# A fused attention and gated-MLP block: how its first rows are normalised, and where two weight loads stand in the queue

## The chip, the cores and the metric

One core of one Trainium2 chip. The metric is the device time of one execution in microseconds (us); the median of several runs is compared. A core has five engines that run side by side, each through its own instructions in the order in which the program lists them: TensorE (PE, matmuls), VectorE (DVE), ScalarE (ACT), GpSimd (POOL) and SyncE (SP, which here issues nearly all DMAs).

## The reference

The input x has 2048 rows of 640. Each row is normalised (mean and variance over its 640 values); everything else works on the normalised rows xn:

```
xn  = (x - mean) / sqrt(var + 1e-5)
# attention in 4 segments of 512 rows, 32 heads of 20, with a memory M, z carried on
q, k, v = xn @ wq, xn @ wk, xn @ wv
p     = softmax(q k^T * scale + mask)            # within a segment
a_mem = (phi(q) M) / (phi(q) z + 1e-6)           # from the segments before
o     = sigmoid(beta) * a_mem + (1 - sigmoid(beta)) * (p v)
M, z += phi(k)^T v, sum phi(k)                   # phi(t) = t + 1 if t > 0 else exp(t)
s   = o @ wo
# gated MLP, inner width 1536
h   = sigmoid(xn @ w_gate) * (xn @ w_up)
out = x + s * silu(h @ w_down)
```

## The kernel before

Work goes segment by segment, 512 rows each (n = 0 to 3). A segment's rows come as four blocks of 128 rows (j = 0 to 3), two to a tile xt2 that has two buffers. For matmuls the kernel needs xn transposed (xnT, five chunks of 128 columns). `Wg` and `Wu`, the gate and up weights, are loaded in three blocks of 512 columns (`load_glu(i, 0)` and `load_glu(i, 1)`, 640 KB each, issued by SP); one block serves four gates or four ups of 128 columns.

Two kinds of code set the order. From segment 0's scores on a planner interleaves attention (`scores`, L516; `weigh`, L534) with due tasks and with `bulk`, the list of gates, ups and downs. What comes ahead of that is written out by hand in `startup` (L573). Every engine keeps the program's order, and SP's DMAs go out in program order too.

`startup` begins with 40 small matmuls on an identity (`warm`, L571), which keep TensorE busy while the first rows arrive. For each of segment 0's four blocks `ln_stats` (L227) takes mean and variance on DVE (two `bn_stats` over 320 columns each, L236 and L237, and an aggregate, L238), and POOL makes the inverse root (add eps L241, power -0.5 L242). `ln_norm` (L248) then normalises on DVE (L253), transposes by five matmuls on PE into one PSUM tile (L260), and ACT copies it out to xnT (L261). As soon as two blocks are there, V's matmuls start (`v_tile`, L356: five matmuls for half the columns of one block; the six half tiles of blocks 0 to 2 are made here). Then come K's five chunks (`k_chunk`, L289) and Q's (`q_chunk`, L321), each five matmuls into one of three PSUM buffers that ACT empties.

K and Q then change their layout through DRAM. `stage_out` (L310) writes three or two chunks of K to the scratch tensor Ks (of Q to Qs); `relay` (L274) reads them back as four DMAs into KT (QT), head by head. `q_bound` makes a bound on the scores that goes the same way through Cs (L345) and is read back by `c_in` (L353) as four DMAs into QT. The first scores need KT, QT from Qs and QT from Cs. Between Q and these scores PE has eight gates and ups, which use block 0 of Wg and Wu; the next ones need block 1. The loads of block 1 stand at L614 and L615, behind the first QT<-Cs issues. The next transposes of segment 1 (by DMA, L263), block 2 of the weights, and the second half's relays follow in the same queue. A DMA's landing semaphore is one of eight that are used in turn, so a DMA waits until the eighth one before it has landed.

Of the kernel before, what the change touches and what calls it, by code (L numbers as in the profile page):

```python
# [9 lines left out]
P = 128  # L10
S = 2048
D = 640
# [17 lines left out]
ACT = mybir.ActivationFunctionType  # L30
ALU = mybir.AluOpType
# [18 lines left out]

NU = len(UNITS)
NSLOT = NG // 2 * NU
WARM = 40
FIRST = 0.45
PASS = [0.41, 0.41, 0.41, 0.2, 0.61]
R = NSLOT / 24
# [3 lines left out]
def kernel(  # L60
# [14 lines left out]
    nc = tc.nc  # L75
# [3 lines left out]
    cpool = ctx.enter_context(tc.tile_pool(name="const", bufs=1))  # L79
# [3 lines left out]
    lnp = ctx.enter_context(tc.tile_pool(name="ln", bufs=2))  # L83
    xpool = ctx.enter_context(tc.tile_pool(name="xpool", bufs=2))
# [4 lines left out]
    fpool = ctx.enter_context(tc.tile_pool(name="fpool", bufs=2))  # L89
# [35 lines left out]
    def later(lag, fn, *a):  # L125
        at(clock[0] + lag * R, 0.0, fn, *a)


    st = [dict() for _ in range(NSEG)]
# [31 lines left out]
    def load_glu(i, which):  # L161
        w, src = ((Wg, B_w_gate), (Wu, B_w_up))[which]
        nc.sync.dma_start(w[i][:], src[:, i * L:(i + 1) * L].rearrange("(c p) n -> p c n", p=P))
# [11 lines left out]

    nhalf = cpool.tile([P, 2], F32, name="nhalf")
    nc.gpsimd.memset(nhalf[:], -0.5)
    ident = cpool.tile([P, P], BF, name="ident")
    nc.gpsimd.memset(ident[:], 0.0)
    nc.gpsimd.affine_select(out=ident[:], in_=ident[:], compare_op=ALU.not_equal, fill=1.0,  # L180
# [46 lines left out]
    def ln_stats(n, p, i0=0, i1=2):  # L227
        s = st[n]
        x = s[f"x{p}"]
        if i0 == 0:  # L230
            s[f"mv{p}"] = lnp.tile([P, 2, 2], F32, name="mv")
            s[f"rstd{p}"] = lnp.tile([P, 2], F32, name="rstd")
        mv, rstd = s[f"mv{p}"], s[f"rstd{p}"]
        for i in range(i0, i1):
            bs = lnp.tile([P, 2, 6], F32, name="bs")
            nc.vector.bn_stats(bs[:, 0, :], x[:, i, 0:HB])  # L236
            nc.vector.bn_stats(bs[:, 1, :], x[:, i, HB:D])  # L237
            nc.vector.bn_aggr(mv[:, i, :], bs[:])  # L238

        def root():  # L240
            nc.gpsimd.tensor_scalar(rstd[:, i0:i1], mv[:, i0:i1, 1], EPS, None, op0=ALU.add)  # L241
            nc.gpsimd.tensor_tensor(rstd[:, i0:i1], rstd[:, i0:i1], nhalf[:, i0:i1], op=ALU.pow)  # L242
        if n <= 1:
            root()
        else:
            later(0.6, root)

    def ln_norm(n, p, i):  # L248
        s = st[n]
        if "xnT" not in s:  # L250
            s["xnT"] = xpool.tile([P, DC, L], BF, name="xnT")
        xn = lnp.tile([P, D], BF, name="xn")
        nc.vector.tensor_scalar(xn[:], s[f"x{p}"][:, i, :], s[f"mv{p}"][:, i, 0:1], s[f"rstd{p}"][:, i:i + 1],  # L253
                                op0=ALU.subtract, op1=ALU.mult)
        j = 2 * p + i
        dst = s["xnT"][:, :, j * P:(j + 1) * P]
        if n == 0:
            pT = dtile([P, DC, P], BF, "pT")
            for c in range(DC):
                nc.tensor.transpose(pT[:, c, :], xn[:, c * P:(c + 1) * P], ident[:])  # L260
            nc.scalar.copy(dst, pT[:])  # L261
        elif n == 1:
            nc.sync.dma_start_transpose(dst, xn[:])  # L263
        else:
            later(0.7, lambda: nc.sync.dma_start_transpose(dst, xn[:]))


    def half_tile(tiles, n, half):
        return tiles[(2 * n + half) % 3]

    def relay(n, half, src, dst):
        rows = src[n % 2].rearrange("(g r d) n -> r d g n", r=4, d=DH)
        for r in range(4):
            nc.sync.dma_start(half_tile(dst, n, half)[32 * r:32 * r + DH, :, :], rows[r][:, 4 * half:4 * half + 4, :])  # L274

    def evacuate(dst, ps):
        if delay[0]:
            nc.vector.tensor_copy(dst, ps)
        else:
            nc.scalar.copy(dst, ps)  # L280

    def k_chunk(n, c):
        s = st[n]
        if c == 0:
            s["k5"] = stg.tile([P, DC, L], BF, name="k5")
            s["kabs"] = stg.tile([P, DC], F32, name="kabs")
# [21 lines left out]
    def stage_out(n, half, src, dst, name):  # L308
        a, b = ((0, 3), (3, 5))[half]
        nc.sync.dma_start(src[n % 2][a * P:b * P, :].rearrange("(c p) n -> p c n", p=P), st[n][name][:, a:b, :])  # L310
        if n:
            later(1.0, relay, n, half, src, dst)
# [255 lines left out]
    def warm(count):  # L568
        ps = dtile([P, L], F32, "wps")
        for i in range(count):  # L570
            nc.tensor.matmul(ps[:, 0:P], lhsT=ident[:], rhs=ident[:], start=True, stop=True)  # L571

    def startup():  # L573
        warm(WARM)
        nc.gpsimd.memset(KT[0][:], 1.0)
        ln_stats(0, 0, 0, 1)
        ln_stats(0, 0, 1, 2)
        ln_norm(0, 0, 0)
        warm(10)
        ln_stats(0, 1, 0, 1)  # L580
        ln_norm(0, 0, 1)
        v_tile(0, 0, 0)
        ln_stats(0, 1, 1, 2)
        v_tile(0, 1, 0)
        ln_norm(0, 1, 0)
        v_tile(0, 0, 1)
        ln_norm(0, 1, 1)
        v_tile(0, 2, 0)
        v_tile(0, 1, 1)
        v_tile(0, 2, 1)  # L590
        v_ones(0, 4)
        make_ind()
        nc.gpsimd.memset(KT[1][:], 1.0)
        for c in range(DC):
            k_chunk(0, c)
        nc.gpsimd.memset(KT[2][:], 1.0)
        stage_out(0, 0, Ks, KT, "k5")
        for c in range(DC):
            q_chunk(0, c)
            if c == 0:  # L600
                stage_out(0, 1, Ks, KT, "k5")
                relay(0, 0, Ks, KT)
            elif c == 2:
                stage_out(0, 0, Qs, QT, "q5")
            if c < 2:
                ln_stats(1, 0, c, c + 1)
        make_bd()
        v_ones(4, 8)
        take(1)
        q_bound(0)  # L610
        relay(0, 0, Qs, QT)
        stage_out(0, 1, Qs, QT, "q5")
        c_in(0, (0,))
        load_glu(1, 0)  # L614
        load_glu(1, 1)  # L615
        ln_stats(1, 1, 0, 1)
        gates()
        take(1)
        ln_norm(1, 0, 0)
        ln_norm(1, 0, 1)  # L620
        take(1)
        ln_stats(1, 1, 1, 2)
        take(5)
        at(0.1, 0.68, v_tile, 0, 3, 0)
        at(0.5, 0.68, v_tile, 0, 3, 1)
        at(R * 2.0, 0.0, ln_norm, 1, 1, 0)
        at(R * 2.3, 0.0, ln_norm, 1, 1, 1)
# [118 lines left out]
    n = NSEG - 1  # L746
# [39 lines left out]
```

## Time and profile before

| | us |
|---|---|
| median of 3 runs | 338.39 (338.29 to 341.84) |
| the profiled execution | 339.99 |
| its span, first to last instruction | 338.3 |
| TensorE busy in it | 326.1 (96%) |
| VectorE, ScalarE, GpSimd busy | 223.9, 226.5, 111.0 |
| first warm matmul | 1.45 |
| first V matmul | 7.38 |
| first K matmul | 12.44 |
| first score matmul | 32.60 |

A row of the timeline gives the start, the length, the engine, the line, the operation, what it writes and reads, how many instructions are merged, and in brackets how long the engine was idle just before and what ended that. A q behind the engine's name (SPq, ACTq) marks its queue: issuing a DMA, not moving its data. When a DMA has landed is told by its semaphore, to which each DMA engine that carried a part of it adds a one. A matmul's end is modelled, so rows of PE overlap a little.

### The profile page before, as it was taken

Reading aid. Unit: us, or ns where it says so; the run is one execution under the profiler, and the core shown is the slowest. Engines: PE = TensorE matmul, PEld = TensorE weight load, DVE = VectorE, ACT = ScalarE, POOL = GpSimd, SP = SyncE. Lnnn points to the kernel's source line nnn. Section 1 sums busy time; section 2 is a strip of 40 time slices with the busy share of each in tenths; the row PEclk is TensorE's granted clock in tenths of the full one; section 3 lists DMA queues with packets and bytes.
Section 4 is the critical chain, followed back from the end, with each engine's and each line's share of the span. In section 5 each row is a group of like instructions: output and inputs, shape, how many; then the busy total and the mean of one; then the engine's idle time right before and its main releaser. Section 6 shows DMA issues by size and latency. Waiting matters only on the chain.

```text
span 338.3 us, 8318 instructions
## 1 busy us (share of the span) xinstructions
PE 326.1 (96%) x3360; PEld 186.5 (55%) x3402; DVE 223.9 (66%) x532; ACT 226.5 (67%) x237; POOL 111.0 (33%) x157
## 2 busy tenths in 40 slices
PE   8999899999999999999999999999999999999995
PEld 7544455445665565554566466554456655544673
DVE  6375356479877577778775977876673687533355
ACT  3653797778786666477876765565887776786730
POOL 6645232232325322332223622333222323233214
PEclk9999999999999999999999999999999999999999
DMA  7956994774840731045730263042220521210032
GB/s 237 343 183 194 265 112 83 234 214 91 186 109 3 131 92 53 20 137 88 203 94 2 54 105 98 21 155 86 74 70 3 83 76 41 63 55 3 2 62 78
DMA packets 54725, 35.53 MB, mean 105 GB/s; under 512 B 28576, under 2 KB 54688, under 8 KB 54688
## 3 DMA queue, kind: packets, MB, share of 16 engines
q1 hardware_dynamic: 52480, 32.23, 37.7%
q10 hardware_dynamic: 2208, 2.79, 2.7%
q8 instruction: 26, 0.43, 0.6%
q14 instruction: 11, 0.09, 0.1%
HBM read 20.19 MB, written 8.39 MB: 84 GB/s over the span
## 4 chain that ended last, share of the span: by engine, by line
PE 87%; DMA 5%; DVE 3%; ACT 2%; issue 1%; POOL 0%; SPq 0%; DVEq 0%; ACTq 0%; POOLq 0%
PE yp L456 14%; PE up L438 14%; PE gp L428 13%; PE Aps L547 9%; PE Sps L522 7%; PE sp L502 6%; PE psk L289 6%; PE psq L321 6%; PE psv L360 6%; DMA Wu<-in_B_w_up_dram 2%; PE wps L571 2%; DMA xnT<-xn 1%; PE dm L388 1%; PE am L410 1%; ACT pt L527 1%
## 5 line engine op out<-in xcount | busy, mean ns | idle before, releaser
L527 ACT ACTIVATE pt<-Sps 128x2048 bf16<-128x2048 f32 x80 | 150.1, 1876 | 24.6 <-PE Sps L522 21.3
L530 POOL TENSOR_SCALAR_AFFINE_SELECT pt<-pt 128x1024 bf16<-128x1024 bf16 (+1 forms) x80 | 76.4, 956 | 197.8 <-ACT pt L527 197.8
L438 PE MATMUL up<-xnT,Wu 128*128 128x512 bf16 x229 | 58.8, 379 | 1.5 <-DVE Mbd L396 0.7
L428 PE MATMUL gp<-xnT,Wg 128*128 128x512 bf16 x221 | 58.0, 379 | 2.1 <-DMA Wg<-in_B_w_gate_dram 0.9
L456 PE MATMUL yp<-Wd,hT 128*128 128x320 bf16 x384 | 57.1, 299 | 0.0
L442 DVE SCALAR_TENSOR_TENSOR hT<-tg,up 128x512 bf16<-128x512 bf16 x48 | 32.7, 681 | 32.1 <-PE up L438 29.2
L431 ACT ACTIVATE tg<-gp 128x512 bf16<-128x512 f32 x48 | 28.6, 597 | 35.4 <-PE gp L428 34.7
L547 PEld LDWEIGHTS <-pt 128*128 128x128 bf16 x1280 | 43.1, 96 | 14.7 <-DVE od L556 2.1
L547 PE MATMUL Aps<-va,pt 128*128 128x21 bf16 x1280 | 44.5, 173 | 0.9 <-DVE od L556 0.8
L456 PEld LDWEIGHTS <-hT 128*128 128x128 bf16 x384 | 35.4, 97 | 15.7 <-issue 2.8
L438 PEld LDWEIGHTS <-Wu 128*128 128x128 bf16 x240 | 21.4, 97 | 24.4 <-issue 3.1
L428 PEld LDWEIGHTS <-Wg 128*128 128x128 bf16 x240 | 20.9, 97 | 22.6 <-issue 1.7
L461 DVE SCALAR_TENSOR_TENSOR aa<-t,yp 128x320 bf16<-128x320 bf16 x32 | 15.4, 482 | 26.7 <-ACT t L459 26.5
L522 PE MATMUL Sps<-QT,KT 24*128 24x128 bf16 (+3 forms) x512 | 32.0, 301 | 0.8 <-ACT pt L527 0.4
L360 PE MATMUL psv<-Wv,xnT 128*128 128x320 bf16 x160 | 26.4, 299 | 0.2
L459 ACT ACTIVATE t<-yp 128x320 bf16<-128x320 f32 x32 | 14.0, 437 | 18.4 <-PE yp L456 17.2
L502 PE MATMUL sp<-Wo,oT 128*128 128x320 bf16 x160 | 25.9, 300 | 0.0
L321 PE MATMUL psq<-xnT,Wq 128*128 128x512 bf16 x96 | 23.6, 380 | 0.6 <-issue 0.5
L289 PE MATMUL psk<-xnT,Wk 128*128 128x512 bf16 x92 | 23.5, 379 | 0.5 <-issue 0.2
L522 PEld LDWEIGHTS <-KT 24*128 24x128 bf16 x512 | 9.3, 92 | 25.5 <-issue 23.9
L504 DVE SCALAR_TENSOR_TENSOR aa<-aa,sp 128x320 bf16<-128x320 bf16 x32 | 15.5, 484 | 9.5 <-PE sp L502 9.5
L502 PEld LDWEIGHTS <-oT 128*128 128x128 bf16 x160 | 14.5, 98 | 8.0 <-issue 2.0
(74 smaller groups left out, 327.3 us busy)
## 6 DMA issues: line engine op xcount, KB each, us to landing
KT<-Ks SPq DMA_DIRECT2D x32, 80.0 KB
QT<-Qs SPq DMA_DIRECT2D x32, 80.0 KB
xr<-in_A_x_dram SPq DMA_DIRECT2D x15, 160.0 KB
out_dram<-xr SPq DMA_DIRECT2D x15, 160.0 KB
xt<-in_A_x_dram SPq DMA_DIRECT2D x6, 320.0 KB
Wg<-in_B_w_gate_dram SPq DMA_DIRECT2D x3, 640.0 KB
Wu<-in_B_w_up_dram SPq DMA_DIRECT2D x3, 640.0 KB
Wd<-in_B_w_down_dram ACTq DMA_DIRECT2D x1, 1920.0 KB
```

Source lines behind the costliest of these rows:

```text
L289: nc.tensor.matmul(ps[:], lhsT=W["k"][:, k, c * P:(c + 1) * P], rhs=s["xnT"][:, k, :], start=(k == 0), stop=(k == DC - 1))
L321: nc.tensor.matmul(ps[:], lhsT=W["q"][:, k, c * P:(c + 1) * P], rhs=s["xnT"][:, k, :], start=(k == 0), stop=(k == DC - 1))
L360: nc.tensor.matmul(ps[:], lhsT=s["xnT"][:, k, j * P:(j + 1) * P], rhs=W["v"][:, k, half * HB:(half + 1) * HB], start=(k == 0), stop=(k == ...
L428: nc.tensor.matmul(gp[:], lhsT=Wg[f // 4][:, k, fo:fo + P], rhs=s["xnT"][:, k, :], start=(k == 0), stop=(k == DC - 1))
L438: nc.tensor.matmul(ps[:], lhsT=Wu[f // 4][:, k, fo:fo + P], rhs=s["xnT"][:, k, :], start=(k == 0), stop=(k == DC - 1))
L442: empty(lambda: nc.vector.scalar_tensor_tensor(out=h[:], in0=tg[:], scalar=1.0, in1=ps[:], op0=ALU.add, op1=ALU.mult))
L456: nc.tensor.matmul(yp[:], lhsT=s["hT"][f][:, j * P:(j + 1) * P], rhs=W["d"][:, f, hs], start=(f == 0), stop=(f == FC - 1))
L502: nc.tensor.matmul(sp[:], lhsT=s["oT"][:, j, c, :], rhs=W["o"][:, c, hs], start=(c == 0), stop=(c == DC - 1))
L522: nc.tensor.matmul(Sps[:, r, c0:c0 + ncol], lhsT=kt[32 * r:32 * r + KR, gi, kb * P:(kb + 1) * P], rhs=qt[32 * r:32 * r + KR, gi, kb * P:L] ...
L527: nc.scalar.activation(pt[:], Sps[:], ACT.Exp, scale=SCALE)
L530: nc.gpsimd.affine_select(out=diag, in_=diag, compare_op=ALU.is_ge, fill=0.0, base=0, pattern=[[0, 4], [0, cnt], [1, P]], channel_multipli ...
L547: nc.tensor.matmul(A[:, qb, r, :], lhsT=pt[:, r, off:off + P], rhs=V[4 * (n % 2) + kb][:, 4 * g + r, :], start=first, stop=True, skip_grou ...
```

## The change

Segment 0's blocks get code of their own. Block 1's statistics move from DVE to ACT: a Copy whose accumulator gives the sum, then a Square with the negative mean as bias whose accumulator gives the sum of squares, then Sqrt. Block 0's statistics stay on DVE, and its root is taken by ACT (Sqrt) too; for both blocks DVE takes the reciprocal ahead of the normalisation. Blocks 2 and 3 keep DVE and POOL. Block 0 is normalised ahead of any other block's statistics on DVE. The order of V's half tiles changes, the first `warm` has 34 matmuls instead of 40, ACT loads its Sqrt table at the start and its Exp table behind V, and POOL's later memsets are held behind the last block by a small copy. The loads of block 1 of Wg and Wu move from behind `c_in` to directly behind K's second staging, ahead of K's relay.

```diff
-WARM = 40
+WARM = 34
...
+    def half_stats(j, h):
...
+        nc.vector.bn_stats(s[f"bs{j}"][:, h, :], s[f"x{j // 2}"][:, j % 2, h * HB:(h + 1) * HB])
+        if h:
+            nc.vector.bn_aggr(s[f"mv{j}"][:], s[f"bs{j}"][:])
+
+    def root_act(j):
+        s = st[0]
+        nc.scalar.activation(s[f"r{j}"][:], s[f"mv{j}"][:, 1:2], ACT.Sqrt, bias=epsb[:])
+
+    def root_pool(j):
+        r = st[0][f"r{j}"][:]
+        nc.gpsimd.tensor_scalar(r, st[0][f"mv{j}"][:, 1:2], EPS, None, op0=ALU.add)
+        nc.gpsimd.tensor_tensor(r, r, nhalf[:, 0:1], op=ALU.pow)
+
+    def sum_act(j):
...
+        nc.scalar.activation(s["sq"][:], s[f"x{j // 2}"][:, j % 2, :], ACT.Copy, accum_out=s["sm"][:, 0:1])
+
+    def square_act(j):
+        s = st[0]
+        nc.scalar.activation(s["sm"][:, 1:2], s["sm"][:, 0:1], ACT.Copy, scale=-1.0 / D)
+        nc.scalar.activation(s["sq"][:], s[f"x{j // 2}"][:, j % 2, :], ACT.Square, bias=s["sm"][:, 1:2],
+                             accum_out=s[f"mv{j}"][:, 1:2])
+        nc.scalar.activation(s[f"r{j}"][:], s[f"mv{j}"][:, 1:2], ACT.Sqrt, scale=1.0 / D, bias=epsb[:])
+
+    def norm_first(j):
...
+        if j < 2:
+            nc.vector.reciprocal(r, r)
...
+        nc.vector.tensor_scalar(xn[:], s[f"x{j // 2}"][:, j % 2, :], mean, r, op0=op, op1=ALU.mult)
+        pT = dtile([P, DC, P], BF, "pT")
+        for c in range(DC):
+            nc.tensor.transpose(pT[:, c, :], xn[:, c * P:(c + 1) * P], ident[:])
+        nc.scalar.copy(s["xnT"][:, :, j * P:(j + 1) * P], pT[:])
+        return xn
...
     def startup():
+        nc.scalar.activation(scr[:, 0:1], epsb[:], ACT.Sqrt)
         warm(WARM)
         nc.gpsimd.memset(KT[0][:], 1.0)
-        ln_stats(0, 0, 0, 1)
-        ln_stats(0, 0, 1, 2)
-        ln_norm(0, 0, 0)
+        sum_act(1)
+        half_stats(0, 0)
+        half_stats(0, 1)
+        root_act(0)
+        square_act(1)
+        norm_first(0)
         warm(10)
-        ln_stats(0, 1, 0, 1)
-        ln_norm(0, 0, 1)
+        half_stats(2, 0)
+        half_stats(2, 1)
+        root_pool(2)
+        norm_first(1)
         v_tile(0, 0, 0)
-        ln_stats(0, 1, 1, 2)
+        half_stats(3, 0)
+        half_stats(3, 1)
+        root_pool(3)
+        v_tile(0, 0, 1)
+        norm_first(2)
         v_tile(0, 1, 0)
-        ln_norm(0, 1, 0)
-        v_tile(0, 0, 1)
-        ln_norm(0, 1, 1)
+        v_tile(0, 1, 1)
+        xn = norm_first(3)
         v_tile(0, 2, 0)
-        v_tile(0, 1, 1)
         v_tile(0, 2, 1)
+        nc.gpsimd.tensor_copy(scr[:, 1:2], xn[:, 0:1])
+        nc.scalar.activation(scr[:, 0:1], epsb[:], ACT.Exp)
         v_ones(0, 4)
...
             if c == 0:
                 stage_out(0, 1, Ks, KT, "k5")
+                load_glu(1, 0)
+                load_glu(1, 1)
                 relay(0, 0, Ks, KT)
...
         c_in(0, (0,))
-        load_glu(1, 0)
-        load_glu(1, 1)
         ln_stats(1, 1, 0, 1)
```

More of the change, by code (lines that the diff above doesn't have):

```diff
@@ L177 @@
     nc.gpsimd.memset(nhalf[:], -0.5)
+    epsb = cpool.tile([P, 1], F32, name="epsb")
+    nc.gpsimd.memset(epsb[:], EPS)
+    scr = cpool.tile([P, 2], F32, name="scr")
     ident = cpool.tile([P, P], BF, name="ident")
@@ L246, in ln_stats @@
             later(0.6, root)
+    def half_stats(j, h):
+        s = st[0]
+        if h == 0:
+            s[f"bs{j}"] = lnp.tile([P, 2, 6], F32, name="bs")
+            s[f"mv{j}"] = lnp.tile([P, 2], F32, name="mv0", bufs=4)
+            s[f"r{j}"] = lnp.tile([P, 1], F32, name="r0", bufs=4)
+        nc.vector.bn_stats(s[f"bs{j}"][:, h, :], s[f"x{j // 2}"][:, j % 2, h * HB:(h + 1) * HB])
[9 more added lines that the diff above has]
+    def sum_act(j):
+        s = st[0]
+        s["sq"] = fpool.tile([P, D], BF, name="aa", bufs=4)
+        s["sm"] = lnp.tile([P, 2], F32, name="sm", bufs=1)
+        s[f"mv{j}"] = lnp.tile([P, 2], F32, name="mv0", bufs=4)
+        s[f"r{j}"] = lnp.tile([P, 1], F32, name="r0", bufs=4)
+        nc.scalar.activation(s["sq"][:], s[f"x{j // 2}"][:, j % 2, :], ACT.Copy, accum_out=s["sm"][:, 0:1])
+    def square_act(j):
+        s = st[0]
+        nc.scalar.activation(s["sm"][:, 1:2], s["sm"][:, 0:1], ACT.Copy, scale=-1.0 / D)
[3 more added lines that the diff above has]
+    def norm_first(j):
+        s = st[0]
+        if j == 0:
+            s["xnT"] = xpool.tile([P, DC, L], BF, name="xnT")
+        r = s[f"r{j}"][:]
+        if j < 2:
+            nc.vector.reciprocal(r, r)
+        xn = lnp.tile([P, D], BF, name="xn")
+        mean, op = (s["sm"][:, 1:2], ALU.add) if j == 1 else (s[f"mv{j}"][:, 0:1], ALU.subtract)
+        nc.vector.tensor_scalar(xn[:], s[f"x{j // 2}"][:, j % 2, :], mean, r, op0=op, op1=ALU.mult)
[4 more added lines that the diff above has]
+        return xn
     def ln_norm(n, p, i):
@@ L256, in ln_norm @@
         dst = s["xnT"][:, :, j * P:(j + 1) * P]
[L257 to L262, printed above, removed]
+        if n == 1:
             nc.sync.dma_start_transpose(dst, xn[:])
```

## The prediction, made before the changed kernel ran

> **What bounds the kernel now.** I read the totals of the profile's page first, then the chain that ended last, then PE's timeline for its idle places, then the SP queue's timeline and the landing updates behind it, then the first 13 us engine by engine.
>
> ```profile
> PE 326.1 (96%) x3360; PEld 186.5 (55%) x3402; DVE 223.9 (66%) x532; ACT 226.5 (67%) x237; POOL 111.0 (33%) x157
> PE 87%; DMA 5%; DVE 3%; ACT 2%; issue 1%; POOL 0%; SPq 0%; DVEq 0%; ACTq 0%; POOLq 0%
> ```
>
> TensorE is the bound: 96% busy. Adding up PE's idle gaps over 30 ns in its timeline gives 8.0 us, of which 1.45 lie before the first matmul; 4.1 us more are the tail. A change of order can win only some of these, or fewer of the 50 warm matmuls. These gaps lie where the change works (PE's timeline, start and duration, idle before in brackets):
>
> ```profile
> 32.60 0.68 PE L522 MATMUL Sps<-QT,KT 24*128 24x512 bf16 x4
> 35.65 1.25 PE L428 MATMUL gp<-xnT,Wg 128*128 128x512 bf16 x4 [0.90 <-DMA Wg<-in_B_w_gate_dram]
> 37.47 1.25 PE L438 MATMUL up<-xnT,Wu 128*128 128x512 bf16 x5 [0.24 <-DMA Wu<-in_B_w_up_dram]
> ```
>
> PE waits 0.90 us for the second gate block and 0.24 for the second up block. A third gap, 0.14 us at 51.16, waits for a transpose that is late in the SP queue. The first scores look free of a wait, but are not: three of the four matmuls start at 32.60, the fourth at 32.90, when the last QT<-Cs has landed (32.85). So the first scores are also set by DMA. The chain by time (start, length, what) says what leads there:
>
> ```profile
> 22.87 3.18 DMA Qs<-q
> 26.87 3.22 DMA QT<-Qs
> 30.10 7.32 DMA Wu<-in_B_w_up_dram
> ```
>
> And the SP queue, whose order the change alters (start, issue time):
>
> ```profile
> 18.65 0.37 SPq L310 DMA_DIRECT2D Ks<-k  x1
> 21.32 1.45 SPq L274 DMA_DIRECT2D KT<-Ks  x4
> 22.87 0.39 SPq L310 DMA_DIRECT2D Qs<-q  x1
> 25.66 0.35 SPq L345 DMA_DIRECT2D Cs<-cb  x1
> 26.06 1.52 SPq L274 DMA_DIRECT2D QT<-Qs  x4
> 27.63 0.38 SPq L310 DMA_DIRECT2D Qs<-q  x1
> 28.11 1.39 SPq L353 DMA_DIRECT2D QT<-Cs  x4
> 29.54 0.39 SPq L163 DMA_DIRECT2D Wg<-in_B_w_gate_dram  x1
> 30.10 1.01 SPq L163 DMA_DIRECT2D Wu<-in_B_w_up_dram  x1
> ```
>
> SP stands idle from 19.02 to 21.32 because K's relay waits for the first Ks to land: its last landing update is at 21.26. Q's first staging (22.87) stands behind the relay, though its data were ready at 21.86; Q's relay starts at 26.06 because Qs landed at 26.05; from there to the last QT<-Cs it is 6.80 us of issues and landings.
>
> **Part 1, the start.** The rows that set it:
>
> ```profile
> 0.78 1.28 ACT L261 ACT_TABLE_LOAD   x1 [0.78 <-PEq L770]
> 5.25 0.45 DVE L253 TENSOR_SCALAR xn<-xt,mv,rstd 128x640 bf16<-128x640 bf16 x1
> 6.64 0.39 DVE L253 TENSOR_SCALAR xn<-xt,mv,rstd 128x640 bf16<-128x640 bf16 x1
> 9.17 0.88 DVE L253 TENSOR_SCALAR xn<-xt,mv,rstd 128x640 bf16<-128x640 bf16 x1 [0.77 <-POOL rstd L242]
> ```
>
> Removed: two bn_stats and an aggregate from DVE for block 1 (0.44 + 0.47 + 0.21), two POOL add+pow pairs (0.23 + 0.57 each), six warm matmuls (107 ns apart in this stretch: 0.64 us). Added on ACT, idle until 6.50 but for the table load: a Copy and a Square over 128x640 (0.69 each, by L261's row), a small Copy and two Sqrt of one column (0.23 each, by the 128x32 tanh), reads of the sums that the trace does not show (0 to 0.3 us each; I take 0.1), and a second table load with an Exp later. On DVE two reciprocals (0.25, by L553).
>
> Block 1 lands at 3.52, so the Copy runs 3.55 to 4.24; block 0's mean and variance are ready at 4.24 as before, its Sqrt ends near 4.6, the reciprocal near 4.9, and xn 0 runs 4.90 to 5.35 instead of 5.25 to 5.70. Meanwhile ACT takes the Square and has block 1's root near 5.9. DVE does block 2's statistics from 5.26 to 6.3, a reciprocal, and xn 1 from 6.55 (6.64 before). Block 3 lands at 6.83 in both. xn 3 starts near 9.1 and takes 0.4 instead of 0.88, since POOL's memsets are held behind it. On PE the first V tile starts near 7.3; its second half must wait for Wv's second half (landed 7.95); from there five V tiles of 0.68 and two transposes of 0.28 end at 11.93 instead of 12.60. So K starts **0.67 us earlier**; 0.1 to 0.9 is what the unknown reads allow.
>
> The second table load falls behind the last V eviction (12.40): 1.28 + 0.23, then K's first eviction at 13.9 where its sum is ready at 13.05. With three PSUM buffers K's fourth chunk needs that buffer free only at 15.17, so it costs nothing. The Trainium skill, "ScalarE: Activation LUTs", section "What ACT_TABLE_LOAD costs", counts a drain of 1.38 us beside the 1.28 us load; the trace has a row of 1.28 and none for a drain. By the Trainium skill K's first buffer would come free near 15.9 and PE would lose 0.7 us here; by the row, nothing.
>
> **But the 0.67 us do not count.** Ks must still land (21.26), and that is ring time: the landing updates, one per DMA engine, show the engines busy without pause from x through the first Wu (ten of them done at 17.0 to 17.5, five at 18.2 to 19.0, the last at 20.25), and Ks behind it. Issued 0.67 earlier, it lands when it did. So relay and Qs are issued as before (21.32, 22.87), Qs cannot land before 26.05, and PE reaches its first scores 0.67 us sooner only to wait. The cover that hides the start's gain, and up to that much of any loss, is this chain. POOL's later memsets (by 0.4 us) have until IK at 19.44 and the relays of the other half at 37.
>
> **Part 2, the loads.** The two issues (0.39 and 1.01 us) move on SP past fifteen DMAs: four K relays, Qs, Cs, four Q relays, the second Qs, four QT<-Cs. Their issue time costs nothing, as it fits into the 2.3 us in which SP waits for Ks; that cover gone, it would be 1.40. On the wait side they win 0.90 + 0.24, and 0.14 at 51.16 since SP is free sooner for the transposes: **1.28 us**.
>
> The price is in the DMA engines. The load rates around the new place:
>
> ```profile
> 20.00:21.00 1.00, 1.00 (x6) 0.48 (x5) 0.97 (x5) 0.59 (x1) 0.00 (x0) 1.00 0.36 122
> 21.00:22.00 1.00, 1.00 (x7) 0.45 (x5) 1.00 (x4) 0.59 (x1) 0.76 (x2) 1.00 0.03 11
> ```
>
> The last two numbers are DMA share and GB/s: idle from about 20.8 to 22. Two blocks of 640 KB need more: behind x's second pair the first Wu took 1.8 us on each engine (15.4 to 17.2). With the second Ks done near 19.9, Wg is done near 21.7 and Wu near 23.5 on ten engines, up to 0.7 later on five, near 25.6 on the slowest. A relay posts ten engine updates, so it uses ten engines; four relays landed 0.55 to 0.7 apart (23.65 to 25.30): 2.3 us. Qs landed 0.75 behind the last. So Qs lands at 23.5 + 2.3 + 0.75 = 26.55 on the common engines, 27.3 on those that lag. If relays that stand queued run at 46 ns a KB row (the usual packet here; eight rows each), it is 1.5 us instead of 2.3, and 25.8 to 26.5. Bounds: below 26.05 it cannot land; if the slowest engine carries relays, 25.6 + 2.3 + 0.75 = 28.6. It probably carries none: in the second half's relays the slowest engine ended the third Wu at 44.65, while the relay behind it had landed everywhere by 43.22. I take **26.9, 0.85 late** (between 26.5 and 27.3).
>
> **Sum.** First scores 0.85 later, then three waits of 1.28 us gone: −0.43 us, on the profiled execution's 339.99 (span 338.3, 1.7 around it) as on the median 338.39, which is the shorter of the two: **338.0**. The point where gain turns to loss is Qs landing at 27.33.
>
> **Rivals.**
> (a) Nothing queues: Qs lands at 26.05 as before, all 1.28 us stay: 337.1. For it: the idle DMA stretch. Against: 1.28 MB at the 350 GB/s of the full stretches is 3.7 us, and only 1.2 us are idle.
> (b) The start counts too: 0.67 + 1.28 = 1.95 off, 336.4. It needs Ks to land earlier, and the queue to be no limit; the updates speak against both.
> (c) Slower: the slowest engine carries the relays. Qs lands at 28.6, scores 2.55 late, less 1.28: +1.27, 339.7. For it: that engine was 1.3 us behind all others at Wu; against: the second half's relays. It decides from 27.33 on.
> (d) PE stands idle before the scores long enough to lose its clock. The first matmuls run at 107 ns a start until 6.47 and at 56 ns from 6.67: about 5.1 us at half pace, 2.6 us lost. Again before the scores, that is 340.6, with (c) 342.3. Against: the unbroken idle would be some 1 us in my forecast, 2 in (c), as the first of the four QT<-Cs lands 1.45 before the last. The Trainium skill, "TensorE: Matmul & The Clock Gate", Part 1, says the clock halves after an idle window of about 3.4 us; by that neither case reaches it. The same rule bears on six warm matmuls fewer and PE's short idles at 5.1 and 6.6: the clock could rise a window later, 1.7 us lost at the start, all but some 0.1 of it hidden by the wait for QT<-Cs.
> (e) The change doesn't do what it says: ACT is no sooner ready with block 1 than DVE was, and xn 1 is not earlier. Then the time is still 338.0, as the start is hidden.
>
> **How the numbers follow.** Forecast (with (e)) 0.55, own range 337.2 to 338.6; (a) 0.15, (b) 0.07, (c) 0.15, (d) and what I have not seen 0.08. The range 336.2 to 340.2 goes from just under (b) to half a us over (c), which leaves out most of (d). About 1% (3.4 us) is what a measurement of this kernel can tell from no change; all cases but (d) with (c) lie within it. Faster by over 1% would need more than all the gaps touched here: 0.04. Slower by over 1%: 0.09. Within: 0.87.
>
> **What would show it.** Right: xn 0 near 4.9, K's first matmul near 11.8; SP issues Wg and Wu near 18.4 to 19.9 and K's relay still near 21.3; Qs lands at 26.5 to 27.3; PE has a new wait for QT<-Cs of 1 to 2 us before L522, and none at the first use of the second Wg and Wu; PE's idle total is nearly as before. Wrong: scores starting at 32 with no wait (b), Qs landing past 27.5 (c), or matmuls of 107 ns after the wait (d).

## The result, and the profile after

| | before | after |
|---|---|---|
| median, us | 338.40 (337.20 to 341.99) | 340.11 (338.82 to 342.21) |
| ratio after to before | | 1.0041, interval 1.0024 to 1.0058 |
| the profiled execution | 339.99 | 339.20 |
| its span | 338.3 | 337.5 |

The forecast was 338.0, 0.4 us shorter than before. The kernel became 1.4 us longer (0.0041 of 338.4; the two medians lie 1.7 apart). That is inside the range, but on the other side of zero. The profiled execution of after is one of the short ones among its runs, and that of before one of the long ones: side by side the two traces show a gain that the medians do not have. Most of what follows is about that.

The totals and the chain's shares, from the page of after:

```profile
PE 328.0 (97%) x3396; PEld 185.9 (55%) x3396; DVE 222.9 (66%) x531; ACT 230.0 (68%) x247; POOL 109.6 (32%) x155
PE 87%; DMA 5%; DVE 4%; ACT 2%; SPq 1%; issue 1%; POOL 0%; DVEq 0%; ACTq 0%
```

PE is still the bound. **The start** went as the prediction had it. ACT's timeline of after (start, length, engine, line, operation), the reading of a sum and the table load:

```profile
4.14 0.19 ACT L276 ACTIVATION_READ_ACCUMULATOR aa<-xt 128x1 f32 x1
...
12.40 1.28 ACT L648 ACT_TABLE_LOAD   x1
13.70 0.20 ACT L648 ACTIVATE scr<-epsb 128x1 f32<-128x1 f32 x1
```

DVE's timeline of after, the first and the last normalisation:

```profile
4.78 0.45 DVE L294 TENSOR_SCALAR xn<-xt,mv,r 128x640 bf16<-128x640 bf16 x1
...
8.91 0.45 DVE L294 TENSOR_SCALAR xn<-xt,mv,r 128x640 bf16<-128x640 bf16 x1 [0.77 <-POOL r L268]
```

The read takes 0.19 us, the next ACTIVATE follows the table load's end by 0.02, and K's first matmul is at 11.76 where 11.8 was forecast. **The loads** stand in SP's queue where the change puts them (SP's timeline of after):

```profile
17.96 0.37 SPq L358 DMA_DIRECT2D Ks<-k  x1
18.38 0.46 SPq L163 DMA_DIRECT2D Wg<-in_B_w_gate_dram  x1
18.89 0.61 SPq L163 DMA_DIRECT2D Wu<-in_B_w_up_dram  x1
20.28 1.47 SPq L322 DMA_DIRECT2D KT<-Ks  x4
21.79 0.39 SPq L358 DMA_DIRECT2D Qs<-q  x1
```

The stretch from 20 to 22 us, in which the DMA engines stood idle before (share 0.36, then 0.03), by windows of after (the last three numbers are granted clock, DMA share and GB/s):

```profile
20.00:21.00 1.00, 1.00 (x6) 0.45 (x5) 0.97 (x5) 0.51 (x2) 0.44 (x2) 1.00 0.87 259
21.00:22.00 1.00, 1.00 (x6) 0.49 (x5) 0.70 (x3) 0.51 (x2) 0.60 (x3) 1.00 1.05 353
```

It is full now, and what was issued behind the loads pays: the chain of after by time shows Q's staging, issued 1.08 us sooner than before (21.79 against 22.87), taking 5.91 us instead of 3.18.

```profile
15.81 4.40 DMA Ks<-k
21.79 5.91 DMA Qs<-q
30.03 3.16 DMA QT<-Cs
```

So Qs lands at 27.70 instead of 26.05. PE's timeline of after, at the three places where before had its waits and its first scores:

```profile
32.72 0.37 PE L570 MATMUL Sps<-QT,KT 24*128 24x512 bf16 x1 [0.73 <-DMA QT<-Cs]
33.32 0.80 PE L570 MATMUL Sps<-QT,KT 24*128 24x512 bf16 x3 [0.23 <-DMA QT<-Cs]
...
35.43 1.24 PE L476 MATMUL gp<-xnT,Wg 128*128 128x512 bf16 x5
...
36.93 1.25 PE L486 MATMUL up<-xnT,Wu 128*128 128x512 bf16 x5
```

The waits for Wg and Wu (0.90 and 0.24) are gone, and a wait for QT<-Cs (0.73 and 0.23) stands ahead of the scores. In this execution the second block's first up is 0.54 us earlier than before (36.93 against 37.47).

### The profile page after: what moved, and what is told of

The parts are those of the page before. It is cut to its first block, busy times and chain, and to the rows that moved or that the text cites. A ratio compares the mean times of both kernels' runs of the same rounds, so it can differ in the third digit from the quotient of the medians.

```text
span 337.5 us, 8356 instructions
## 1 busy us (share of the span) xinstructions
PE 328.0 (97%) x3396; PEld 185.9 (55%) x3396; DVE 222.9 (66%) x531; ACT 230.0 (68%) x247; POOL 109.6 (32%) x155
## 4 chain that ended last, share of the span: by engine, by line
PE 87%; DMA 5%; DVE 4%; ACT 2%; SPq 1%; issue 1%; POOL 0%; DVEq 0%; ACTq 0%
PE gp L476 15%; PE up L486 14%; PE yp L504 14%; PE Aps L595 9%; PE Sps L570 7%; PE psv L408 7%; PE sp L550 6%; PE psk L337 6%; PE psq L369 5%; DMA Qs<-q 2%; PE dm L436 1%; DMA Ks<-k 1%; PE am L458 1%; ACT pt L575 1%; DMA QT<-Cs 1%; SPq L322 1%
## 5 line engine op out<-in xcount | busy, mean ns | idle before, releaser
L575 ACT ACTIVATE pt<-Sps 128x2048 bf16<-128x2048 f32 x80 | 150.1, 1876 | 26.1 <-PE Sps L570 22.8
L486 PE MATMUL up<-xnT,Wu 128*128 128x512 bf16 x240 | 59.7, 379 | 0.7 <-DVE Mbd L444 0.7
L476 PE MATMUL gp<-xnT,Wg 128*128 128x512 bf16 x240 | 59.6, 379 | 0.1
L479 ACT ACTIVATE tg<-gp 128x512 bf16<-128x512 f32 x48 | 28.6, 596 | 34.0 <-PE gp L476 34.0
L369 PE MATMUL psq<-xnT,Wq 128*128 128x512 bf16 x100 | 24.3, 380 | 0.0
L337 PE MATMUL psk<-xnT,Wk 128*128 128x512 bf16 x100 | 24.2, 379 | 0.0
```

The costliest lines, as they stand in the source:

```text
L369: nc.tensor.matmul(ps[:], lhsT=W["q"][:, k, c * P:(c + 1) * P], rhs=s["xnT"][:, k, :], start=(k == 0), stop=(k == DC - 1))
L476: nc.tensor.matmul(gp[:], lhsT=Wg[f // 4][:, k, fo:fo + P], rhs=s["xnT"][:, k, :], start=(k == 0), stop=(k == DC - 1))
L486: nc.tensor.matmul(ps[:], lhsT=Wu[f // 4][:, k, fo:fo + P], rhs=s["xnT"][:, k, :], start=(k == 0), stop=(k == DC - 1))
L575: nc.scalar.activation(pt[:], Sps[:], ACT.Exp, scale=SCALE)
```

## The experiments

Three theories were tested. **T1**: the loads, put ahead, cost more in the DMA engines than the prediction took, and push Qs and the scores back. **T2**: the wait ahead of the scores also makes PE lose its clock (rival (d)), in part of the executions. **T3**: before's profiled waits of 1.14 us were unusually long, so that there was less to win. All ratios are to before on the same chip, with 95% intervals. The runs are numbered e1 to e18.

### Each half of the change alone

The loads alone are before with L614 and L615 moved:

```diff
                 stage_out(0, 1, Ks, KT, "k5")
+                load_glu(1, 0)
+                load_glu(1, 1)
                 relay(0, 0, Ks, KT)
...
         c_in(0, (0,))
-        load_glu(1, 0)
-        load_glu(1, 1)
```

> Only the two loads move; the start is as before. Theory T1 (the wait is moved, and the clock plays no part): Qs lands at 27.3 to 27.8 instead of 26.05, the first scores start 1.2 to 1.7 us later, the waits for the second Wg and Wu (0.90 + 0.24 in the profile of before) are gone; median against before between 0 and +0.5 us. Theory T2 (the difference between the medians, +1.7 us, is TensorE's clock: more executions of the changed kernel lose a stretch of 3.4 us at half clock, and they lose it through the idle places of the new start): no more executions at a mean clock of 0.996 or less than before has, median within 0.5 us of before. Theory T3 (the waits for Wg and Wu in the one profile of before are not there in most executions, so there was little to win, and the moved loads only cost): median +1.0 to +1.7 us at a mean clock like before's.

The start alone is after with the two lines in their old place.

> Only the start is changed; the loads stand where they were. T1: K's first matmul near 11.8, but Qs lands at 26.0 and the first scores start near 32.6 as before; median within 0.4 us of before. T2 (clock lost through the new start's idle places): 3 or more executions in 10 at a mean clock of 0.996 or less, median +1 us or more. T3: median within 0.5 us of before, clock as before.

Loads alone (e1): **1.0084 [1.0058, 1.0110]**; the scores wait 1.26 and 0.33 us. Start alone (e2): **1.0004 [0.9989, 1.0020]**; the scores start at 32.20 and the wait for Wu is back with 0.90. So the whole loss comes with the loads, and the start is worth nothing by itself, as the prediction said. None of the three forecasts for the loads alone held: the largest was 1.7 us, and it is 2.8 (0.0084 of 338.6), with four of only six executions at the lowered clock that is shown below.

### Both kernels again, unchanged

> The kernel before once more, for a second profile and the clock of its executions. T1 and T2: the waits of 0.90 and 0.24 us for Wg and Wu are there again. T3: they are below 0.3 us in sum, and the span is near 336.7, the median less 1.7. T2 wants at most 2 executions in 10 at a mean clock of 0.996 or less.

> The changed kernel once more, for a second profile and the clock of its executions (8 of 22 were at 0.995 or less, and those took 340.4 to 342.2; the rest 338.8 to 341.0). T1: first scores at 32.7 to 33.3 with an idle PE of 1 us in front. T2: if this execution is one of the slow ones, the clock row shows 3.4 us at half pace either in the first 10 us or around the wait before the first scores (32 to 36 us); the place says which of the two idle places costs.

> The changed kernel, a third profile. Theory C: if the time is 341 or more, the clock row has a stretch of 3.4 us at 0.5 that starts between 33 and 38 us; if it is below 340.5, none. Theory Q: a time of 341 or more comes with a wait for QT<-Cs of 3 us or more.

> The changed kernel, a fourth profile; the same as for the third.

> The kernel before, a third profile. If its first two profiles overstate the waits: a span near 336.9, waits for Wg and Wu of 0.5 us or less in sum, first up of block 1 near 36.3. If they are ordinary: waits of 0.6 to 1.2 us, first up at 37.0 or later, and the span's difference lies elsewhere.

> The kernel before, a fourth profile; the same as for the third.

Timed again, before (e3) stands to itself at 1.0004 [0.9984, 1.0023] and after (e4) at 1.0052 [1.0028, 1.0077]. With these there are four traces of each. The table takes from each the time at which Q's relay is issued (Qs has landed), PE's waits ahead of the scores and for Wg and Wu, the start of V's matmuls, which follow the scores, and the first up of the second block:

| | Q's relay | wait, scores | V starts | wait, Wg + Wu | first up | execution |
|---|---|---|---|---|---|---|
| before, the first | 26.06 | none | 33.22 | 0.90 + 0.24 | 37.47 | 339.99 |
| before, e3 | 26.28 | none | 33.27 | 0.42 + 0.24 | 37.03 | 339.43 |
| before, e16 | 27.70 | none | 34.29 | 0 + 0.37 | 37.60 | 339.07 |
| before, e17 | 26.28 | none | 32.89 | 1.29 + 0.24 | 37.53 | 339.01 |
| after, the first | 27.72 | 0.73 + 0.23 | 34.06 | none | 36.93 | 339.20 |
| after, e4 | 27.98 | 0.96 + 0.12 | 34.30 | none | 37.17 | 338.57 |
| after, e14 | 28.44 | 1.21 | 35.00 | none | 37.88 | 340.20 |
| after, e13 | 28.34 | 1.26 + 0.27 | 34.93 | none | 39.43 | 342.05 |

"None" means no idle row. The four score matmuls take 0.40 us where all their data has landed (e17), and 0.68, 0.76 and 1.12 in before's other traces: part of the wait for QT<-Cs lies inside that row, so V's start is the fairer measure. In the mean V starts at 33.42 in before and at 34.57 in after, 1.15 later.

**T3 falls**: the waits for Wg and Wu are 0.37 to 1.53 us in before's traces, 0.93 in the mean, and the first profile's 1.14 is ordinary. For **T1**: Q's relay is at 28.1 in the mean instead of 26.6. One trace of before, e16, has it at 27.70 with no load ahead; there K's relay was issued at 22.72 already, against 21.32 to 21.42 in the others, so a late K does that too. (Its waits of 0.37 meet the sign that was named for T3, its first up at 37.60 the sign against.) And e13 against e14 shows **T2**: both wait about equally long, V starts at nearly the same time, and e13's first up comes 1.55 us later. PE's timeline of e13:

```profile
33.68 0.37 PE L570 MATMUL Sps<-QT,KT 24*128 24x512 bf16 x1 [1.26 <-DMA QT<-Cs]
...
34.93 1.94 PE L408 MATMUL psv<-Wv,xnT 128*128 128x320 bf16 x10
36.67 2.34 PE L476 MATMUL gp<-xnT,Wg 128*128 128x512 bf16 x5
...
39.43 1.25 PE L486 MATMUL up<-xnT,Wu 128*128 128x512 bf16 x5
```

The same rows in e14:

```profile
33.81 1.26 PE L570 MATMUL Sps<-QT,KT 24*128 24x512 bf16 x4 [1.21 <-DMA QT<-Cs]
35.00 1.53 PE L408 MATMUL psv<-Wv,xnT 128*128 128x320 bf16 x10
36.37 1.24 PE L476 MATMUL gp<-xnT,Wg 128*128 128x512 bf16 x5
...
37.88 1.25 PE L486 MATMUL up<-xnT,Wu 128*128 128x512 bf16 x5
```

Five gates of equal size take 2.34 us in e13 and 1.24 in e14. The same window of both (PE busy and its matmuls come second; the clock is the third number from the end), first e13, then e14:

```profile
35.90:39.32 3.42, 3.42 (x18) 1.17 (x15) 0.42 (x1) 1.72 (x3) 0.68 (x1) 0.50 0.92 290
```

```profile
35.90:39.32 3.42, 3.42 (x37) 1.69 (x36) 0.57 (x2) 3.07 (x4) 0.68 (x1) 1.00 0.75 240
```

Eighteen matmuls instead of 37 at clock 0.50, for 3.41 us. Such a stretch lowers an execution's mean clock to 0.995 or less, so that it can be counted in executions without a trace too: 27 of 54 with both loads ahead and nothing to fill the wait (after, e1, e6), 4 of 127 of before. In the 22 runs of after, the eight that have it have a median of 341.77, the fourteen others 339.72.

The traces' records of the granted clock show when this happens. In all twenty traces the time from a rise of the clock to its next fall is a whole multiple of 3.413 us: 30.72 (nine times) from the first rise to the fall behind the wait, in e13 and in the run with three blocks ahead (e8), 331.09 (97 times) in most others; and the lowered stretch in both lasts 3.41. So the clock is set anew on a grid of 3.41 us, whose edges lie at another place in each execution (the first rise is at 4.5 to 7.4 us). In e13 the window before the fall, 32.49 to 35.90, holds the whole wait, the scores, each of which uses 24 of the 128 rows, and only 0.97 us of matmuls over all 128 rows (V's, from 34.93). In e14 the edges lie at 30.69 and 34.10, and the window that has the wait in it also has 1.91 us of gates and ups ahead of it. Over all full-clock windows of the twenty traces, the 22 that end in a fall, most of them in the tail of the kernel, hold at most 1.15 us of 128-row matmuls, and the 1916 others at least 1.46. No run varied this on purpose, so that it is the share of such matmuls that decides is read from this split alone.

### Filling the wait

12 or 24 small matmuls on the identity at the end of `startup`, ahead of the scores:

```diff
+        warm(24)   # the other kernel: warm(12)
```

> The changed kernel with 24 more small matmuls on the identity (1.34 us at 56 ns) between the eighth gate/up and the first scores, where TensorE otherwise stands idle for about 1 us. Theory C (clock: in half of the executions the idle time in front of the scores drops TensorE to half clock for one stretch of 3.4 us, 1.7 us lost): hardly any execution at 0.996 or less; median 0.5 to 1.2 us below the changed kernel's, about 339.5. Theory Q (queueing alone: the wait for QT<-Cs is longer in the slow executions, the lower mean clock goes with it but does not cost): median as the changed kernel's, 340.3 or more, since matmuls on the identity bring no data sooner.

> The changed kernel with 12 matmuls on the identity (0.67 us) in front of the first scores; the 24 of the run before (1.34 us) kept the clock in all but one execution but were longer than the wait itself. Theory C (a drop to half clock costs some 2 us in half of the executions): at most 2 in 12 at 0.996 or less, ratio 1.002 to 1.004, spread of the times under 3 us. Theory Q (the lower mean clock is a mark of a long wait and costs nothing of its own): ratio as the changed kernel's, 1.004 to 1.005, or above.

PE's timeline with 12:

```profile
31.99 0.83 PE L619 MATMUL wps<-ident 128*128 128x128 bf16 x12
33.49 1.06 PE L570 MATMUL Sps<-QT,KT 24*128 24x512 bf16 x4 [0.67 <-DMA QT<-Cs]
```

24 (e5) gave **1.0051 [1.0023, 1.0080]**, and the gain that was expected is missed. It is not that they outlast the wait: in the trace they run from 32.22 to 33.7, the last QT<-Cs lands at 34.06, and V starts at 34.42, within after's 34.06 to 35.00. 12 (e12) gave **1.0037 [1.0017, 1.0057]**. Executions with a lowered clock are gone but for one of 24 (27 of 54 without the fill): the idle of PE is what lowers it. The time that this saves is not shown by these ratios, whose intervals overlap with after's, and both fill traces lose 1.2 and 1.5 us at a place near 195 us that no other trace has (below). What the loads cost without T2 is better read from after's fourteen runs at full clock, 1.3 us above before.

### Another queue, and how much is loaded ahead

The same two loads at the same place, issued by ACT instead of SP:

```diff
+                load_glu(1, 0, nc.scalar)
+                load_glu(1, 1, nc.scalar)
```

> The changed kernel with the two loads issued at the same place from ScalarE's DMA queue instead of SP's. If the order within SP's queue on each DMA engine is what makes Qs late (queue theory): Qs lands at 26.0 to 26.8, the scores wait 0.3 us or less, no execution at 0.996 or less, median 0.5 to 1.5 us below before, 337.2 to 338.2. If it is the DMA engines' total rate (rate theory): Qs lands at 27.5 or later as in the changed kernel, median 340 or more.

ACT's queue in its timeline:

```profile
19.20 0.41 ACTq L163 DMA_DIRECT2D Wg<-in_B_w_gate_dram  x1
19.65 0.62 ACTq L163 DMA_DIRECT2D Wu<-in_B_w_up_dram  x1
```

**1.0052 [1.0021, 1.0082]** (e6): Q's relay at 28.62, the scores wait 1.16 us. K's relay and Qs stand in a queue of their own here and are as late as behind the loads. It is not the order in SP's queue; the DMA engines have 1.28 MB more to move in that time, whoever issues it.

One block fewer, run twice (`load_glu(1, 1)` back in its old place), and one more (`load_glu(2, 0)` ahead as well):

> The changed kernel with only the gate block's load moved ahead; the up block's stands behind c_in as before. Queue theory: half the data in front, Qs lands 1.8 us sooner than with both, near 26.2 to 26.5; scores wait 0.6 to 1.0 us; no wait for Wg, 0 to 0.3 us for Wu; few executions (2 in 10 at most) at 0.996 or less; median between before and 0.8 us below it. Rate theory: the same. Theory C with a threshold near 0.7 us of idle time: still 4 in 10 at 0.996 or less, median 339.5.

> The changed kernel with only the gate block's load ahead, once more (0.9988, interval 0.9963 to 1.0012 the first time). Queue theory with the clock: ratio 0.996 to 1.000, at most 1 execution in 12 at 0.996 or less; Qs near 26.3 and the scores waiting 0.3 us or less in the profile.

> The changed kernel with a third block of 640 KB (the third gate block) moved in front of K's relay as well. Queue theory: Qs lands another 1.8 us later (29.5 to 30), the wait in front of the scores grows to 2.5 to 3 us. Theory C: then 8 in 10 executions or more are at 0.996 or less, the trace shows a stretch of 3.4 us at half clock that begins at or behind the wait (32 to 38 us), with starts 107 or 430 ns apart instead of 56 and 216; median 1.8 + 0.5 to 1 us above the changed kernel's, 342.3 to 343.3. Without C (Q alone): 1.8 us above, and no matmuls at half pace after 8 us.

| blocks ahead | Q's relay | wait, scores | executions at a lowered clock | ratio |
|---|---|---|---|---|
| none (e2) | 25.98 | none | 0 of 12 | 1.0004 [0.9989, 1.0020] |
| one (e7) | 26.35 | none | 0 of 12 | 0.9988 [0.9963, 1.0012] |
| one (e11) | 26.39 | 1.08 | 0 of 12 | 0.9986 [0.9965, 1.0007] |
| two (after, e4) | 27.72, 27.98 | 0.96, 1.08 | 14 of 34 | 1.0041 [1.0024, 1.0058], 1.0052 [1.0028, 1.0077] |
| three (e8) | 30.45 | 3.63 + 0.23 | 5 of 5 | 1.0107 [1.0074, 1.0140] |

The first block costs Q's relay 0.4 us, the second about 1.7 (28.1 in the mean of after's four traces), the third 2.3: the first fits into the idle stretch, the others push all of their time on. In e11 a wait of 1.08 us stands between the second and the third score matmul although Q's relay is on time, against the 0.3 that was expected, and why that QT<-Cs landed late was not followed up. It did not lower the clock: from the last up to V there are 1.96 us without 128-row matmuls, which leaves at least 1.45 of them in any window of 3.41. PE's timeline with three:

```profile
35.69 0.37 PE L570 MATMUL Sps<-QT,KT 24*128 24x512 bf16 x1 [3.63 <-DMA QT<-Cs]
36.29 0.84 PE L570 MATMUL Sps<-QT,KT 24*128 24x512 bf16 x3 [0.23 <-DMA QT<-Cs]
```

Here an idle of 3.6 us lowered the clock in every execution (in the trace 0.50 from 36.10 for 3.41 us).

### What the waits are worth

Both kernels with the second block's loads left out; the matmuls that would use it read block 0 instead, so the output is not the reference's.

```diff
+    Wg[1], Wu[1] = Wg[0], Wu[0]
...
-        load_glu(1, 0)
-        load_glu(1, 1)
```

> The kernel before without the loads of block 1 of Wg and Wu; gates and ups 4 to 7 use block 0 instead, so that part of the product is another one. It measures what the waits for these loads are worth in ordinary executions. If they are worth what the profiles of before show (0.9 + 0.24 + 0.14 in the first, 0.42 + 0.24 in the second): 0.7 to 1.3 us below before. If the profiled executions overstate them (theory T3): 0.0 to 0.6 us below before. In both, no execution at 0.996 or less beyond what before has.

> The changed kernel without the loads of block 1 (block 0 used instead, as in the run beside it). With it the price of the loads in front of the relays is seen by itself. Queue theory with the clock: Qs lands near 26.0, scores start near 32.5 with a wait of 0.3 us or less, no execution at 0.996 or less; 1.2 to 2.0 us below the changed kernel's ratio to before (1.004 to 1.005), so 0.995 to 0.999; and within 0.5 us of the kernel before without these loads, as the start's gain waits for Qs.

Before without them (e9): **0.9962 [0.9942, 0.9982]**; after without them (e10): **0.9966 [0.9945, 0.9987]**. PE's timeline of the first has neither wait:

```profile
32.63 0.39 PE L523 MATMUL Sps<-QT,KT 24*128 24x512 bf16 x4
...
34.32 1.24 PE L429 MATMUL gp<-xnT,Wg 128*128 128x512 bf16 x5
...
35.83 1.25 PE L439 MATMUL up<-xnT,Wu 128*128 128x512 bf16 x5
```

So in before these two loads cost 0.0038 of 339, which is 1.3 us (forecast 1.28 for the three waits). The waits for Wg and Wu alone are 0.93 of it in the mean of before's traces; the rest would be the scores, as V starts at 32.95 here and at 33.42 in the mean of before. The two kernels are alike without the loads: the start is hidden. Two blocks ahead cost after 1.0041 or 1.0052 less 0.9966, which is 2.5 to 2.9 us, against the 1.3 us that they save.

### Only what fits

Half a gate block (256 columns, 320 KB) ahead of K's relay, then the up block and the other half in the old place:

```diff
-    def load_glu(i, which):
+    def load_glu(i, which, c0=0, c1=L):
...
-                load_glu(1, 0)
-                load_glu(1, 1)
+                load_glu(1, 0, 0, 2 * P)
...
         c_in(0, (0,))
+        load_glu(1, 1)
+        load_glu(1, 0, 2 * P, L)
```

> The changed start, and of block 1 only the first half of the gate block (256 columns, 320 KB, used by gates 4 and 5) in front of K's relay; the up block and the gate block's second half behind c_in, in this order. Queue theory: 0.9 us of the engines' time fits into their idle stretch (20.8 to 22), Qs lands at 26.0 to 26.4, scores wait 0.5 us or less, the up block lands before its use at 36; ratio 0.996 to 0.999, no execution at 0.996 or less beyond what before has. If any load in front costs as much as it gives: 0.999 to 1.002.

> Half the gate block in front, once more (0.9972, interval 0.9953 to 0.9992 the first time). Queue theory: 0.995 to 0.999 again, at most 1 execution in 12 at 0.996 or less. If the first was chance: an interval that holds 1.000 well inside.

**0.9972 [0.9953, 0.9992]** (e15) and, run again, **0.9986 [0.9970, 1.0002]** (e18): 0.5 to 0.95 us below before. The first interval excludes 1.000, the second just holds it. PE's timeline of the second:

```profile
32.65 0.40 PE L570 MATMUL Sps<-QT,KT 24*128 24x512 bf16 x4
...
34.35 1.24 PE L476 MATMUL gp<-xnT,Wg 128*128 128x512 bf16 x5
...
35.85 1.25 PE L486 MATMUL up<-xnT,Wu 128*128 128x512 bf16 x5
```

No wait is left, neither for QT<-Cs nor for the weights; the rows lie within 0.03 us of those without the loads. The first of the two traces is less clean: its Qs lands at 26.70, its four scores take 0.74 us, and its first up is at 36.66, though no idle row is left there either. Two gates need only half of the block, and the rest has their time to land.

### A second place that differs

The traces allow one more comparison. ACT's 80 exps over a score tile (128x2048, L575; L527 in before) follow each other in all kernels alike, so their starts show where executions part. From the 17th on:

| | 17th exp | 17th to 77th | span |
|---|---|---|---|
| before: first, e3, e16, e17 | 89.14, 88.58, 89.17, 89.08 | 220.76, 220.73, 219.80, 219.80 | 338.3, 337.7, 337.4, 337.3 |
| after: first, e4, e14 | 88.41, 88.64, 89.34 | 220.70, 219.81, 220.73 | 337.5, 336.8, 338.5 |
| after, e13 (lowered clock) | 90.90 | 221.04 | 340.3 |
| loads alone (e1), by ACT (e6) | 89.66, 89.38 | 219.82, 220.89 | 337.9, 338.6 |
| no loads: e9, e10 | 87.30, 87.36 | 219.80, 221.12 | 335.6, 337.0 |
| half a block: e15, e18 | 88.13, 87.32 | 220.78, 220.37 | 337.2, 336.0 |
| start alone e2, one block e7, e11 | 88.27, 87.69, 88.46 | 220.36, 220.37, 220.83 | 337.0, 336.4, 337.7 |
| three blocks, e8 (lowered clock) | 92.59 | 220.78 | 341.7 |
| with a fill: e5 (24), e12 (12) | 88.77, 88.83 | 220.99, 222.04 | 338.1, 339.3 |

The first column is the work of the change, and its order is that of the ratios in the main, though after's first two lie below three or all of before's. The second column jumps, by 0.6 to 1.3 us, at one place behind the 17th exp. SP's and DVE's timelines of after, which has it:

```profile
84.18 2.08 SPq L426 DMA_TRANSPOSE pkt<-k  x1
86.31 0.57 SPq L358 DMA_DIRECT2D Qs<-q  x1
```

```profile
89.47 0.29 DVE L421 TENSOR_SCALAR q<-q 128x512 bf16<-128x512 bf16 x1 [0.57 <-DMA Qs<-q]
```

SP's and DVE's timelines of e4, the same kernel, which has it not:

```profile
84.42 1.20 SPq L426 DMA_TRANSPOSE pkt<-k  x1
85.66 0.94 SPq L358 DMA_DIRECT2D Qs<-q  x1
```

```profile
89.24 0.29 DVE L421 TENSOR_SCALAR q<-q 128x512 bf16<-128x512 bf16 x1
```

SP needs 2.65 us instead of 2.14 for these two issues, a DVE step on q waits for that staging, and ACT's next exp and PE follow. It is there in before and after (two of four, three of four traces), with the loads and without, and it is why one profile is no median. By it e9 and e10 differ by 1.4 us in span, though their medians are 337.98 and 338.08. Whether it is chance is open: of all fourteen traces with the new start twelve have it, of the six with the old start two.

The two fill kernels have a third place, at their 45th exp, which costs 1.2 and 1.5 us and is in none of the eighteen other traces. There DVE waits for a transpose, and PE for DVE (e5's timelines of DVE and PE):

```profile
194.48 0.45 DVE L306 TENSOR_SCALAR xn<-xt,mv,rstd 128x640 bf16<-128x640 bf16 x1 [1.91 <-DMA xnT<-xn]
195.88 1.25 PE L486 MATMUL up<-xnT,Wu 128*128 128x512 bf16 x4 [1.03 <-DVE om L466]
```

Why the fill brings it was not looked into.

## Why the prediction was right and wrong

**Right.** *The start*: 11.76 against 11.8 forecast, each read 0.19 (0 to 0.3 was allowed, 0.1 taken), nothing lost at the table load. The Trainium skill, "ScalarE: Activation LUTs", "What ACT_TABLE_LOAD costs", would have had a drain of 1.38 us there; the trace does not agree, the next ACTIVATE starting 0.02 us behind the load. *The start does not count*: shown by e2 (1.0004) and by e9 and e10 being alike. Its reason was only half right: Ks did not land at a fixed time (K's relay is at 20.28 to 22.29 in four traces of after), but Qs did not land sooner for it. *The three waits are worth 1.28 us*: 1.3 by e9, and PE's timeline of after has no gap near 51 any more; the size is right, though the waits for Wg and Wu alone are 0.93 in the mean of before's traces, so that it came out this well is in part luck. *The new wait*: for QT<-Cs, 1.0 to 1.5 us, within the 1 to 2 that were named.

**Wrong: the price of the loads in the DMA engines, "26.9, 0.85 late".** This term of the sum was too small. Qs landed at 27.70 in the first trace and at 28.1 in the mean, 1.65 and 2.05 later than in the profile of before, and 1.5 later than its mean; of the forecast's values only the upper bound, 28.6 with rival (c), lies beyond. The steps of that term in the first trace: Wu was done on most engines near 24.2 instead of 23.5, K's four relays at 25.29 to 26.86, where 25.8 was forecast for the last, and Qs 0.84 behind. Every step was late by a little, and none ran at the faster rate that was half allowed for. Rival (c)'s mechanism, one slow engine, was not what did it: Wu's sixteen updates lie between 24.07 and 24.80, so the engines as a whole had too much to move.

That the first trace nevertheless has its scores only 0.84 late (V at 34.06 against 33.22), just as the sum has it, is luck: from Qs to the last QT<-Cs it took 6.00 us instead of 6.80, and the two errors cancel. In the mean of four traces each V starts 1.15 later, and the waits saved are 0.93: a small loss where a gain of 0.43 was forecast. The point of decision, Qs at 27.33, was passed in every trace of after, but the first trace gained 0.54 us at the first up all the same.

**Wrong: rival (d) set aside at 0.08 together with all that was unseen.** The sum charges a wait ahead of the scores with its length alone. The prediction argued that an idle of 1 us, or 2, could not lower the clock. It leant on the Trainium skill, "TensorE: Matmul & The Clock Gate", Part 1, by which it takes an idle window of about 3.4 us. The measurement differs: 1.26 + 0.27 us of idle, with 0.37 us of score matmul in between, were followed by 3.41 us at clock 0.50, and by the mean clock half of the executions with both loads ahead have such a stretch. It costs 1.55 us at the first up in e13, 2.0 in the medians (2.6 was rival (d)'s price), so by estimate about 0.8 us of the mean of after. The same Part 1 of that page of the Trainium skill says that the window runs free, independently of the kernel; the traces agree, with their grid of 3.41 us at another place in each execution. That fits half of the executions: from the last up to V there are 2.1 to 2.5 us without 128-row matmuls in after's traces, and it depends on the edges whether one window takes in nearly all of it, as in e13, or two share it.

**What stays open.** Without the lowered clock the runs of after are still 1.1 to 1.3 us longer than before (339.72 against 338.4 to 338.6; so the clock is not all of it). Five traces with both loads ahead and full clock have their 17th exp at 89.1 in the mean, before's four at 89.0: that explains 0.1. These traces lie on the short side of their kernels' runs and before's on the long side, and the place at 84 us moves each by 0 to 1.3. If SP's slow issue were usual in after and unusual in before, its 0.9 us would account for nearly all of the rest. It is more frequent in the traces with the new start, but the start alone is no longer than before (1.0004), and e9 and e10 have equal medians; executions without a trace cannot show it, and it was not tested. That the loads are the cause is shown (e1, e2, e7, e10); through which place the last 1 us runs is not.

## What to carry to other kernels

A load that is moved ahead to win a wait pays with the landing of everything that the DMA engines move behind it, in whichever queue it is issued; size it to the stretch in which the engines stand idle, here half a block instead of two. A wait that is moved to a place where PE has nothing else to do can cost a stretch of half clock on top of its length, in some executions only, and the mean clock of many runs shows it where one trace may not; look at how much dense matmul is left around the wait, and not at the wait alone. When two traces are compared, find the places where they part first, since one of them may have nothing to do with the change.

## What the runs showed of the hardware

- The granted clock fell to 0.50 for 3.41 us behind idles of 1.26 and 0.27 us (e13), a mean clock of 0.995 or less stands in about half of the executions with both loads ahead (27 of 54), and in 5 of 5 with a wait of 3.63 us. With 12 small matmuls in the wait (0.83 us) it is in 0 of 12, with 24 in 1 of 12.
- The clock changed only on a grid of 3.41 us. It fell behind windows with at most 1.15 us of matmuls over 128 rows (22 of 22), and behind none of the 1916 windows with 1.46 us or more.
- Loads issued by ACT delayed SP's transfers as much as loads in SP's own queue: Q's relay at 28.62 against 27.72 to 28.44.
- Two issues on SP, a transpose and a staging, took 2.1 us in some executions and 2.6 to 2.9 in others of the same kernels (before and after), with 0.9 to 1.3 us on the span behind it.
- Reading an accumulated sum on ACT is an instruction of its own of 0.19 us; a reciprocal of one column on DVE takes 0.11 to 0.16 us.
